# Windowed attention and a gated product: scores issued with values two groups back, weight sums on GpSimd, outputs through other buffers

## The chip, the cores and the metric

The kernel runs on one core of a Trainium2 chip. The metric is the device time of one execution in microseconds (us). Before the change the median of three runs is 662.41 us (660.27 to 663.85). Engines are named as in the profile: PE is TensorE (PEld its weight loads), DVE VectorE, ACT ScalarE, POOL GpSimd, SP SyncE, which issues nearly all DMAs.

## The reference

Attention for 4 batches, 8 heads, 768 positions of 64, with a local window and 24 block summaries, then a gated product of three weights over all 3072 tokens, in float32:

```python
k_sum = k.reshape(B, H, 24, 32, D).max(axis=3)
v_sum = v.reshape(B, H, 24, 32, D).mean(axis=3)
scores_l = where(abs(i - j) < 16, q @ k.T / 8, -1e9)
scores_s = q @ k_sum.T / 8 + log(32)
a = softmax(concatenate([scores_l, scores_s], axis=-1))
attn = a @ concatenate([v, v_sum], axis=2)
x = attn.transpose(0, 2, 1, 3).reshape(3072, 512)
out = ((x @ w_a) * (x @ w_b)) @ w_out        # 512 -> 1536 -> 512
```

## The kernel before

**Numbers in two parts.** TensorE multiplies rounded float32 (`F32R`). Each weight and each activation is kept as a rounded part (hi) and a rest (lo), and a product is three matmuls: hi x hi, lo x hi, hi x lo.

**Chunks.** The tokens form nine chunks u = 0 to 8 of 128-position groups: three of two groups for batch 0, two of three groups for each of batches 1 to 3. For u = 0 to 6 `item(n, u, f)` does one twelfth f of the hidden width: 24 up-products (L1178, 12 for `h0` = x w_a, 12 for `h1` = x w_b, each of 128x384 for a chunk of three groups), then a *gate*: ScalarE copies `h0` to `g` (L1275), VectorE multiplies `h1` by it (L1278), ScalarE rounds that to `gh` (L1280), VectorE forms the rest `gl` (L1283). Nine output products (L1292) follow, six with `gh` and three with `gl`. TensorE does the 24 up-products of the next item before the nine output products of this one.

**Attention of later chunks** (`attention`, `scores`, `transposes`, `products`) runs between items, one group of 128 queries at a time. SyncE loads queries in 16 pieces (`blocks`) into one half of `qin`; VectorE turns them into `qT` (L1122). TensorE forms the scores in banks `c0`, `c1` (L740). VectorE adds the mask (L765) and takes the maximum (L773) into `sbuf`, ScalarE exponentiates (L787), VectorE inverts the sums (L807), GpSimd multiplies by them (L822). VectorE turns the weights into `pbuf` by blocks of 32 (L868). TensorE multiplies by the value window `vbuf` (L890), whose result is split into hi and lo (L934, L938). `lead` joins the value products of a group to the scores of the next one: TensorE does both in one *burst*.

**The last stage** (`whole`) does chunks 7 and 8 together, with seven products of half-size blocks instead of eight. For it `mixtures(f)` forms four sums of weight blocks (T1 to T4) for each of the twelve f: GpSimd adds hi and lo (L1352) and forms sums (L1392), ScalarE rounds them (L1374), GpSimd forms the rest (L1377), and SyncE stores them and three unmixed blocks to `comb` in DRAM (L1336). Two slots, in `S1` and in `late`, are used in turn. Values of chunks 6 to 8 go unrounded to `rawd` or to buffers; `bring_back` loads chunk 6 again and splits it.

**What sets the order.** `Work.emit` plays the operations on a clock of its own with the costs given to `act`, `dve`, `pool`, `pe` and `load`, and issues on each engine the ready operation of the lowest rank. For the first part the order is written out by hand in `ORDER`; an engine's list is followed until it is used up, and operations marked `aside` come only after it. `PLACES` and `MIXED` say at which item a group of attention or a mixture becomes known. On the chip every engine takes its queue strictly in that order.

Of the kernel before, what the change touches and what calls it, by code (L numbers as in the profile page):

```python
# [9 lines left out]
F32 = mybir.dt.float32  # L10
# [59 lines left out]
        434 654-657 660-665 1199 612 638 625 1200 1201 651 669-671 1203 672 1204-1206 717 710  # L70
        675-678 1208 679 680 1209-1211 1213-1216 773 766 1220-1222 1217 1224-1227 827 820
        1229-1232 1234-1237 963 970 1238 1043 1050
# [27 lines left out]
class Work:  # L100
# [10 lines left out]
    def add(self, engine, rank, takes, then, reads, writes, fn, rate=0):  # L111
# [3 lines left out]
            engine=engine, rank=rank, takes=takes, then=then, rate=rate, fn=fn, left=0,  # L115
# [20 lines left out]
    def emit(self):  # L136
# [5 lines left out]
        while any(ready.values()):  # L142
# [34 lines left out]
def attention_moe(  # L177
# [10 lines left out]
    nc = tc.nc  # L188
# [16 lines left out]
    WHOLE, RAW, SPLIT = NU - 2, NU - 3, 5  # L205
# [86 lines left out]
    rawd = dram.tile([3 * WIDE, P, 512], F32, tag="raw", name="rawd")  # L292
# [423 lines left out]
    def scores(u, t, qT, qk, s, sk, banks, diag=None, lead=None):  # L716
# [42 lines left out]
        for h in range(2):  # L759
            if u > FILL:  # L760
                rank = rank_of(u, t) - 0.1 + 0.02 * h
# [15 lines left out]
        for h in range(2):  # L777
            if u > FILL:
                rank = rank_of(u, t) - 0.1 + 0.02 * h
# [3 lines left out]
            for c in range(NP):  # L783
                act(
                    rank, 0.385, [f"{mk}m{h}", xk[h]],
# [42 lines left out]
    def transposes(u, t, s, sk, banks, diag=None):  # L828
# [24 lines left out]
        sv = sbuf.rearrange("p h c x -> p (h c) x")  # L853
# [5 lines left out]
        halves = [slice(0, 4), slice(4, 8)] if u >= SPLIT else [slice(0, 8)]  # L859
# [13 lines left out]
    def products(u, t, vw, vk, bk, pt=None, other=None):  # L873
# [5 lines left out]
        if u >= RAW:  # L879
            other = None  # L880
# [15 lines left out]
        def kept():  # L896
            if u > WHOLE:
                halved(t - chunks[u][1], ps)
                return
            raw, key = slot("S1", 3)  # L900
            act(
                CHAIN, 0.6, [bk], [key],
                lambda: nc.scalar.copy(
                    out=raw.rearrange("p (c a b) -> p c a b", c=NP, a=2),
                    in_=ps.rearrange("p c (b a) -> p c a b", a=2),
                ),
            )
            i = 3 * (u - RAW) + t - chunks[u][1]
            load(80, 262.0, 200, [key], [f"raw.{i}"], rawd[i], raw)
# [42 lines left out]
    SK = ["s0", "s1"]  # L952
    PT = [f"pt{i}{j}" for i in range(4) for j in range(4)]
# [131 lines left out]
    def attention(u):  # L1085
# [4 lines left out]
        if t0 == 0:  # L1090
            prep_keys(b)
            if b < B - 1:
                prep_values(b)
            if b == B - 2:
                work.aside = True
                prep_values(b + 1)
                work.aside = False
# [64 lines left out]

    def later():
        for u in range(FILL + 2, NU):
            yield from attention(u)
        yield
# [32 lines left out]
    def item(n, u, f):  # L1199
# [64 lines left out]
        else:  # L1264
# [5 lines left out]
            for nm, ps, hk in (("a", pa, ak), ("b", pb, bk)):  # L1270
# [6 lines left out]
                CHAIN, 0.08 + W / 1000, [*gk, bk], [bk],  # L1277
# [4 lines left out]
                CHAIN, 0.08 + W / 1000, [bk, ghk], [glk],  # L1282
# [22 lines left out]
        if f == NF - 1:  # L1305
            for j in range(m):
                ob, key = slot("S0" if u < FILL else "S1", j)
                after = CHAIN if u < FILL else 0.5
                if j % 2 == 0:
                    act(after, 0.6, [ok[j]], [key], lambda ob=ob, j=j: nc.scalar.copy(  # L1310
                        out=straight(ob), in_=woven(bank[ok[j]])
                    ))
                else:
                    dve(
                        after, 0.6, [ok[j]], [key],
                        lambda ob=ob: nc.vector.tensor_copy(
                            out=straight(ob), in_=woven(bank[ok[1]])
                        ),
                    )
                row = row0 + j * P  # L1320
                load(90, 262.0, 200, [key], (), out[row : row + P, :], ob)
# [8 lines left out]
    MIXED = [(3, 1), (3, 4), (4, 0), (4, 2), (4, 4), (4, 6), (5, 0), (5, 2), (5, 4), (6, 0), (6, 2), (6, 4)]  # L1330
# [12 lines left out]
    def mixtures(f):  # L1343
        r = [
            spaces["S1"][:, i * 512 : (i + 1) * 512].rearrange("p (h c x) -> p h c x", h=2, c=2)
            for i in range(2)
        ]
        RK = ["S1.0", "S1.1"]
        for i, nm in enumerate("ab"):
            pool(  # L1350
                60, 1.3, weight_key(f, nm), [RK[i], f"go{f}"],
                lambda i=i, nm=nm: nc.gpsimd.tensor_tensor(  # L1352
                    out=r[i].rearrange("p h c x -> p (h c) x"), in0=weight(f, nm)[:, :, 0].bitcast(F32),
                    in1=weight(f, nm)[:, :, 1].bitcast(F32), op=ALU.add,
                ),
            )

        for op, nm in ((B11, "a"), (B21, "a"), (B22, "b")):
            half = op in (B21, B22)
            move(  # L1360
                100, 262.0, 400, weight_key(f, nm) + [f"go{f}"], [f"comb{f}.{op}"], lambda op=op: comb[f][op],
                lambda nm=nm, half=half: flat(f, nm)[:, half * 512 : half * 512 + 512].bitcast(F32),
            )
        def out_part(j, i, h, op):
            def own():
                if j:
                    return late[0][:, 3].rearrange("p c x -> p (c x)")
                return spaces["S1"][:, 1024:1536].bitcast(F32R)

            def w(part):  # L1370
                return own().rearrange("p (c t x) -> p c t x", c=2, t=2)[:, :, part]

            x, key = lambda: r[i][:, h], ["S0.3" if j else "S1.2"]
            act(59, 0.36, [RK[i]], key, lambda: nc.scalar.copy(out=w(0), in_=x()))  # L1374
            pool(
                59, 0.72, [RK[i]], key,
                lambda: nc.gpsimd.tensor_tensor(  # L1377
                    out=w(1), in0=x(), in1=w(0).bitcast(F32), op=ALU.subtract
                ),
            )  # L1380
            move(
                99.5, 262.0, 400, key, [f"comb{f}.{op}"], lambda: comb[f][op],
                lambda: own().bitcast(F32),
            )

        for n, (x, y, z, op, dst) in enumerate((
            ((1, 1), (1, 1), (1, 0), ALU.subtract, T3), ((1, 0), (1, 0), (0, 0), ALU.subtract, T1),
            ((0, 0), (1, 1), (0, 0), ALU.add, T2), ((0, 1), (0, 1), (0, 0), ALU.subtract, T4),
        )):
            pool(  # L1390
                60, 0.72, RK, [RK[x[0]]],
                lambda x=x, y=y, z=z, op=op: nc.gpsimd.tensor_tensor(  # L1392
                    out=r[x[0]][:, x[1]], in0=r[y[0]][:, y[1]], in1=r[z[0]][:, z[1]], op=op
                ),
# [372 lines left out]
```

## Time and profile before

| | |
|---|---|
| median of three runs | 662.41 us |
| profiled execution, its span | 661.2 us, 659.5 us |
| TensorE busy, weight loads busy | 641.8 us (97%), 591.3 us (90%) |
| VectorE, ScalarE, GpSimd busy | 467.0, 275.5, 235.9 us |
| TensorE waiting for `gh` (L1280) | 7.6 us |
| TensorE waiting for transposes (L868) | 2.4 us |

Items of three groups run from about 200 us, the bursts spoken of below from 269 to 513 us, and the last stage from 529 us. A row of a timeline gives start, duration, engine, line and operation, out<-in, the number merged into it, and in brackets the idle time before with what ended it.

### The profile page before, as it was taken

Reading aid. Unit: us, or ns where it says so; the run is one execution under the profiler, and the core shown is the slowest. Engines: PE = TensorE matmul, PEld = TensorE weight load, DVE = VectorE, ACT = ScalarE, POOL = GpSimd, SP = SyncE. Lnnn points to the kernel's source line nnn. Section 1 sums busy time; section 2 is a strip of 40 time slices with the busy share of each in tenths; the row PEclk is TensorE's granted clock in tenths of the full one; section 3 lists DMA queues with packets and bytes.
Section 4 is the critical chain, followed back from the end, with each engine's and each line's share of the span. In section 5 each row is a group of like instructions: output and inputs, shape, how many; then the busy total and the mean of one; then the engine's idle time right before and its main releaser. Section 6 shows DMA issues by size and latency. Waiting matters only on the chain.

```text
span 659.5 us, 13990 instructions
## 1 busy us (share of the span) xinstructions
PE 641.8 (97%) x5064; PEld 591.3 (90%) x5064; DVE 467.0 (71%) x1050; ACT 275.5 (42%) x812; POOL 235.9 (36%) x346
## 2 busy tenths in 40 slices
PE   8999999999999999999999999799999999999997
PEld 6898888899989999998999998699989999999997
DVE  3789988987776694677688865669888645455550
ACT  3996865523533441443345424234454422221120
POOL 6320030246431685357543445214553021212110
PEclk9999999999999999999999999899999999999999
DMA  9999954554433457545345654525546076666620
GB/s 213 266 231 297 335 121 115 125 121 112 117 77 91 115 137 200 128 132 154 125 137 153 175 125 127 149 56 161 176 127 224 11 250 199 197 194 196 198 84 33
DMA packets 184126, 101.98 MB, mean 155 GB/s; under 512 B 138616, under 2 KB 154232, under 8 KB 184056
## 3 DMA queue, kind: packets, MB, share of 16 engines
q1 hardware_dynamic: 183912, 100.95, 56.4%
q8 instruction: 40, 0.66, 0.4%
q14 instruction: 30, 0.25, 0.1%
q10 hardware_dynamic: 144, 0.13, 0.1%
HBM read 71.00 MB, written 30.03 MB: 153 GB/s over the span
## 4 chain that ended last, share of the span: by engine, by line
PE 71%; DVE 15%; SPq 5%; ACT 4%; issue 2%; DMA 2%; POOL 1%; ACTq 0%; DVEq 0%
PE h L1178 29%; PE o L1292 15%; DVE pt L868 10%; PE c L1527 6%; PE h L1527 6%; PE o L1639 5%; SPq L359 4%; PE o L890 3%; PE c L740 2%; PE h L1639 2%; DVE h L1278 2%; ACT s L787 1%; DVE gl L1283 1%; DMA comb<-S 1%; DMA space<-in_q_dram 1%
## 5 line engine op out<-in xcount | busy, mean ns | idle before, releaser
L1178 PE MATMUL h<-x,w 128*128 128x384 f32 (+2 forms) x1608 | 295.7, 320 | 0.1
L1178 PEld LDWEIGHTS h<-x,w 128*128 128x128 f32 x1608 | 253.8, 190 | 9.8 <-issue 1.0
L868 DVE STREAM_TRANSPOSE pt<-s 32x128 f32<-32x128 f32 (+1 forms) x372 | 123.8, 333 | 15.9 <-POOL s L822 9.0
L1292 PE MATMUL o<-w,gh 128*128 128x512 f32 x396 | 100.1, 389 | 7.7 <-ACT gh L1280 7.6
L822 POOL TENSOR_TENSOR s<-s,nml 128x480 f32<-128x480 f32 x40 | 43.8, 1096 | 149.6 <-DVE nml L807 148.3
L1292 PEld LDWEIGHTS o<-w,gh 128*128 128x128 f32 x396 | 72.8, 191 | 19.7 <-ACT gh L1280 10.5
L787 ACT ACTIVATE s<-s,nml 128x120 f32<-128x120 f32 x160 | 61.4, 386 | 21.4 <-DVE nml L773 21.3
L1178 PE MATMUL h<-late,w 128*128 128x384 f32 x192 | 62.8, 327 | 0.0
L1280 ACT CAST gh<-h 128x384 fp32r<-128x384 f32 x48 | 22.9, 476 | 90.9 <-DVE h L1278 90.9
L671 POOL TENSOR_TENSOR S<-S 96x256 f32<-96x256 f32 (+3 forms) x58 | 33.1, 572 | 34.7 <-DMA S<-in_v_dram 26.6
L1292 PE MATMUL o<-w,gl 128*128 128x512 f32 x162 | 45.5, 387 | 0.0
L1278 DVE TENSOR_TENSOR h<-h,g 128x384 f32<-128x384 f32 x48 | 27.0, 563 | 21.4 <-PE h L1178 19.5
L1178 PEld LDWEIGHTS h<-late,w 128*128 128x128 f32 x192 | 36.4, 190 | 0.7
L1392 POOL TENSOR_TENSOR S<-S 128x256 f32<-128x256 f32 x48 | 35.6, 741 | 1.9
L1283 DVE TENSOR_TENSOR gl<-h,gh 128x384 fp32r<-128x384 f32 x48 | 26.4, 550 | 13.7 <-ACT gh L1280 13.0
L1292 PEld LDWEIGHTS o<-w,gl 128*128 128x128 f32 x162 | 30.7, 192 | 5.1 <-issue 0.8
L1592 POOL TENSOR_TENSOR g<-pt,s 128x384 f32<-128x384 f32 x12 | 12.0, 1004 | 63.0 <-ACT s L1579 26.3
L1527 PE MATMUL c<-w,w 128*128 128x384 f32 x180 | 33.8, 326 | 0.0
L1527 PE MATMUL h<-w,w 128*128 128x384 f32 x180 | 33.7, 326 | 0.0
L1352 POOL TENSOR_TENSOR S<-w 128x512 f32<-128x512 f32 x24 | 30.3, 1276 | 7.4 <-DMA out_dram<-S 6.9
L1275 ACT COPY g<-h 128x384 f32<-128x384 f32 x48 | 22.9, 478 | 19.7 <-PE h L1178 19.2
L1527 PEld LDWEIGHTS c<-w,w 128*128 128x128 f32 x180 | 30.3, 189 | 0.7
(213 smaller groups left out, 1031.3 us busy)
## 6 DMA issues: line engine op xcount, KB each, us to landing
w<-comb SPq DMA_DIRECT2D x84, 256.0 KB, 3.0
comb<-w SPq DMA_DIRECT2D x36, 256.0 KB, 2.8
raw<-in_moe_w_a_dram SPq DMA_DIRECT2D x12, 512.0 KB, 6.6
raw<-in_moe_w_out_dram SPq DMA_DIRECT2D x12, 512.0 KB, 6.6
raw<-in_moe_w_b_dram SPq DMA_DIRECT2D x12, 512.0 KB, 7.5
comb<-S SPq DMA_DIRECT2D x24, 256.0 KB, 2.6
comb<-late SPq DMA_DIRECT2D x24, 256.0 KB, 2.4
out_dram<-S SPq DMA_DIRECT2D x22, 256.0 KB, 2.4
```

Of the source, the lines that this page charges most:

```text
L671: lambda: nc.gpsimd.tensor_tensor(out=out, in0=i0, in1=i1, op=ALU.add),
L787: lambda h=h, c=c, sums=sums: nc.scalar.activation(s[h][:, c, :], x[h][:, c, :], AF.Exp, bias=m[:, 0, h, c : c + 1], scale=1.0, accum_out= ...
L822: lambda h=h, r=r: nc.gpsimd.tensor_tensor(out=s[h], in0=s[h], in1=r[:, :, None].broadcast_to([P, NP, KN]), op=ALU.mult,),
L868: lambda js=js, qs=qs, rs=rs: nc.vector.transpose(out=pv[js, rs, qs], in_=sv[qs, rs, js]),
L1178: nc.tensor.matmul(ps, w[:, c, part, :], (xt[:, 4 * xpart : 4 * xpart + 4] if both else inputs_of(u, xpart))[:, :, c].rearrange("p g (a b) ...
L1278: lambda: nc.vector.tensor_tensor(out=pb, in0=pb, in1=g, op=ALU.mult),
L1283: lambda: nc.vector.tensor_tensor(out=gl, in0=pb, in1=gh.bitcast(F32), op=ALU.subtract),
L1292: nc.tensor.matmul(bank[ok[j]], (gh if first else gl)[:, j * P : (j + 1) * P], w[:, :, part, :].rearrange("p (z a) n -> p z n a", a=2), st ...
L1352: lambda i=i, nm=nm: nc.gpsimd.tensor_tensor(out=r[i].rearrange("p h c x -> p (h c) x"), in0=weight(f, nm)[:, :, 0].bitcast(F32), in1=weig ...
L1392: lambda x=x, y=y, z=z, op=op: nc.gpsimd.tensor_tensor(out=r[x[0]][:, x[1]], in0=r[y[0]][:, y[1]], in1=r[z[0]][:, z[1]], op=op),
L1527: nc.tensor.matmul(bank[bk][:, :HT], w[:, c, part, :], x[xpart][:, :, c0 + c].rearrange("p g (a b) -> p g b a", a=2), start=(c, part, xpar ...
L1639: nc.tensor.matmul(bank[bk][:, : nz * CV // 2], gated(x, h)[0][gpart]()[:, js], m, start=(x == 0 and (gpart, part) == (0, 0)), stop=(x == ...
```

## The change

- **Bursts.** For chunks 5 to 8 `groups` takes the place of `attention`. A burst holds the scores of group k and the values of group k-2; the transposes of group k-1 follow it. Softmax has two buffers in turn, `sbuf` and a half of `S1`. In each batch the first scores of the batch have the last values of chunk 4 beside them or none, the second scores have none, and the last two values stand alone. Between bursts inside a batch stand two items; before, two and a half or three. Queries use the first half of `qin` alone. `softmax` and `chunks_of` are small helpers.
- **Transposes** are done in whole rows of 8 blocks, no longer in two halves. Values of chunk 5 are no longer split by key rows.
- **Mixtures.** GpSimd alone forms each sum from the differences of the parts and rounds it; the two slots are used in turn from f = 2 on, one before.
- **Outputs** of chunks 3 to 5 leave through `kin` (first and third group) and the second half of `qin` (second group), which raw values of chunk 7 use as well. Chunk 6's values are split at once; `bring_back` is gone.
- **Planner.** Gates, exponentials and the stores of mixtures get other costs (`slack` delays what another engine does after them), and places and ranks differ. `ORDER` loses the entries of operations that come later.

```diff
@@ Work.emit
+                late = end + (op.slack if o.engine != op.engine else 0.0)
-                o.est = max(o.est, start + op.takes + same if o.engine == op.engine else end)
+                o.est = max(o.est, start + op.takes + same if o.engine == op.engine else late)
@@ attention_moe
-    WHOLE, RAW, SPLIT = NU - 2, NU - 3, 5
+    WHOLE, RAW = NU - 2, NU - 2
@@ scores
-                    rank, 0.385, [f"{mk}m{h}", xk[h]],
+                    rank, 0.575 if u > FILL + 1 else 0.385, [f"{mk}m{h}", xk[h]],
@@ transposes
-        sv = sbuf.rearrange("p h c x -> p (h c) x")
+        sv = (sbuf if sk is SK else sbuf1).rearrange("p h c x -> p (h c) x")
-        halves = [slice(0, 4), slice(4, 8)] if u >= SPLIT else [slice(0, 8)]
+        halves = [slice(0, 4), slice(4, 8)] if False else [slice(0, 8)]
@@ products
-        if u >= RAW:
+        if u > FILL + 2:
             other = None
-            raw, key = slot("S1", 3)
+            raw, key = qin[:, :, P:], "q1.0"
...
+    def softmax(t):
+        if t % 2 == 0:
+            return [sbuf1[:, h] for h in range(2)], ["S1.0", "S1.1"]
+        return s0, SK
...
+    def groups():
+        seq = [(u, i) for u in range(FILL + 3, NU) for i in range(WIDE)]
+        waiting, banks = [], ["c0", "c1"]
...
+        def turned(u, t):
+            b = chunks[u][0]
+            bring(b, t)
+            transposes(u, t, *softmax(t), banks)
+            waiting.append(products(u, t, vbuf, VK, "o3"))
+
+        def direct():
+            reads, bk, fn, split = waiting.pop(0)
+            pe(-1, 1.1, reads, bk, fn)
+            split()
+
+        for k, (u, i) in enumerate(seq):
...
+            for c in range(NP):
+                blocks(98, f"q0.{c}", qin[:, c, :P], q, b, c, t * P)
+            dve(
+                rank_of(u, t) - 0.5, 0.62, [f"q0.{c}.{r}" for c in range(NP) for r in range(0, P, 32)], ["qT"],
+                lambda: nc.vector.transpose(out=qTs, in_=qin[:, :, :P]),
+            )
+            joined = lead.pop() if k == 0 else waiting.pop(0) if t > 1 else None
+            scores(u, t, qTs, "qT", *softmax(t), banks, lead=joined)
+            if t:
+                turned(*(chunks_of(u, t - 1), t - 1))
+            yield
+            if t == S // P - 1:
+                direct()
+                turned(u, t)
+                direct()
...
@@ item
-                CHAIN, 0.08 + W / 1000, [*gk, bk], [bk],
+                CHAIN, 0.56, [*gk, bk], [bk],
...
+                if FILL < u < WHOLE - 1:
+                    ob, key = kin[:, :CV], "kin0.0"
+                if j == 1 and FILL < u < WHOLE - 1:
+                    ob, key = qin[:, :, P:], "q1.0"
...
@@ mixtures
+        def mix(out, x, y, op, reads=()):
             pool(
-                60, 1.3, weight_key(f, nm), [RK[i], f"go{f}"],
+                60, 0.75, reads, [tk],
+                lambda: nc.gpsimd.tensor_tensor(out=out, in0=x(), in1=y(), op=op),
+            )
+        for n, op in enumerate((T1, T3, T2, T4)):
+            if op in (T1, T3):
+                x, y = (("b", 0), ("a", 0)) if op == T1 else (("b", 1), ("b", 0))
+                mix(t, part(*x, 0), part(*y, 0), ALU.subtract, keys)
+                mix(u, part(*x, 1), part(*y, 1), ALU.subtract, keys)
+                mix(t, lambda: t, lambda: u, ALU.add)
+            elif op == T2:
+                mix(u, part("a", 0, 0), part("a", 0, 1), ALU.add, keys)
+                mix(t, lambda: t, lambda: u, ALU.add)
+            else:
+                mix(u, part("a", 1, 0), part("a", 1, 1), ALU.add, keys)
+                mix(t, lambda: u, lambda: t, ALU.subtract)
...
-            act(59, 0.36, [RK[i]], key, lambda: nc.scalar.copy(out=w(0), in_=x()))
+            pool(59, 0.5, [tk], [key], lambda half=half: nc.gpsimd.tensor_copy(out=half(0), in_=t))
...
+            work.ops[-1].slack = 2.0
```

ScalarE around 413 to 426 us of the trace before: L1374 rounds a weight sum into one of the two slots, L1280 is the cast `gh`, L1275 the copy `g`, L903 keeps the values of a group.

```order
L1374 CAST S_191<-S_191 128x2x128
L1280 CAST gh<-h_78 128x384
L1275 COPY g<-h_77 128x384
L1374 CAST late<-S_191 128x2x128
L1280 CAST gh<-h_78 128x384
L903 COPY S_191<-o_76 128x512
L787 ACTIVATE s,nml_172<-s,nml_172 128x120 x4
```

After, at the end of chunk 4 (lines have other numbers there: L1335 is `gh`, L1330 the copy `g`, L934 a rounded value, L1374 the copy of an output into `kin`).

```order
L1335 CAST gh<-h_78 128x384
L1330 COPY g<-h_77 128x384
L934 CAST x<-o_76 128x512
L1335 CAST gh<-h_78 128x384
L1330 COPY g<-h_77 128x384
L934 CAST x<-o_76 128x512
L1374 COPY kin<-o_73 128x512
L1335 CAST gh<-h_78 128x384
L1330 COPY g<-h_77 128x384
L1374 COPY kin<-o_75 128x512
```

No rounding of weight sums stands between the gates; the second copy into `kin` follows the first by three entries.

GpSimd, most of one mixture (f = 5) before: L1352 adds the parts, L1392 forms sums, L1377 the rests, L822 normalises a softmax.

```order
L1352 TENSOR_TENSOR S_191<-w_940 128x512
L1352 TENSOR_TENSOR S_191<-w_995 128x512
L1392 TENSOR_TENSOR S_191<-S_191 128x256
L822 TENSOR_TENSOR s<-s,nml_172 128x4x120 x2
L1377 TENSOR_TENSOR S_191<-S_191 128x2x128
L1392 TENSOR_TENSOR S_191<-S_191 128x256 x2
L1377 TENSOR_TENSOR late<-S_191,late 128x2x128
L1377 TENSOR_TENSOR S_191<-S_191 128x2x128
L1392 TENSOR_TENSOR S_191<-S_191 128x256
```

After, the first half of a mixture (f = 3): L1415 are sums and differences, L1443 the cast into a slot, L1446 the rest, L820 the normalisation.

```order
L1415 TENSOR_TENSOR S_191<-w_899,w_762 128x256 x2
L1415 TENSOR_TENSOR S_191<-S_191 128x256
L1443 CAST late<-S_191 128x2x128
L1446 TENSOR_TENSOR late<-S_191,late 128x2x128
L820 TENSOR_TENSOR s<-s,nml_172 128x4x120
L1415 TENSOR_TENSOR S_191<-w_899 128x256 x2
L1415 TENSOR_TENSOR S_191<-S_191 128x256
L820 TENSOR_TENSOR s<-s,nml_172 128x4x120
L1443 CAST S_191<-S_191 128x2x128
L1446 TENSOR_TENSOR S_191<-S_191 128x2x128
```

The cast into a slot now stands in the same queue as the normalisation, and ahead of it.

VectorE, a group in the middle before: L773 the maximum, L807 the inverse, L868 the transposes, L1278 and L1283 the gate.

```order
L773 TENSOR_REDUCE nml_171<-s 128x4
L1122 STREAM_TRANSPOSE qT<-qin 128x512
L1283 TENSOR_TENSOR gl<-h_78,gh 128x384
L807 RECIPROCAL nml_171<-nml_171 128x4
L868 STREAM_TRANSPOSE pt<-s 32x4x32 x3
L807 RECIPROCAL nml_171<-nml_171 128x4
L868 STREAM_TRANSPOSE pt<-s 32x4x32 x5
L1278 TENSOR_TENSOR h_78<-h_78,g 128x384
L868 STREAM_TRANSPOSE pt<-s 32x4x32 x3
L1283 TENSOR_TENSOR gl<-h_78,gh 128x384
L868 STREAM_TRANSPOSE pt<-s 32x4x32 x13
```

After, a group of batch 3 (L763 mask, L771 maximum, L805 inverse, L866 transposes, L1204 the queries, L1333 and L1338 the gate).

```order
L763 SCALAR_TENSOR_TENSOR S_191<-c_79,mask 128x4x120
L771 TENSOR_REDUCE nml_171<-S_191 128x4
L763 SCALAR_TENSOR_TENSOR S_191<-c_80,mask 128x4x120
L771 TENSOR_REDUCE nml_171<-S_191 128x4
L866 STREAM_TRANSPOSE pt<-s 32x8x32 x3
L1333 TENSOR_TENSOR h_78<-h_78,g 128x384
L805 RECIPROCAL nml_171<-nml_171 128x4
L1204 STREAM_TRANSPOSE qT<-qin 128x512
L1338 TENSOR_TENSOR gl<-h_78,gh 128x384
L866 STREAM_TRANSPOSE pt<-s 32x8x32 x4
```

The transposes between the gates read the other buffer (`s`) than the scores just masked (`S`).

## Rows read from the trace of the kernel before

**Rows 1.** Windows, 275 to 526 us: busy us by engine, clock, DMA share, GB/s.

```profile
275.00:526.00 251.00, 240.74 (x2010) 222.61 (x2010) 191.68 (x511) 107.25 (x365) 107.97 (x128) 0.99 0.47 137
```

**Rows 2.** Waits of PE: us in total, times, longest us.

```profile
PE o L1292 <- ACT gh L1280: 7.6, 8, 4.4
PE o L890 <- DVE pt L868: 2.4, 5, 0.6
```

**Rows 3.** Timeline, 413 to 426 us, SP and ACT.

```profile
413.29 9.65 SPq L359 DMA_DIRECT2D qin<-in_q_dram  x16
...
423.04 0.38 SPq L1336 DMA_DIRECT2D comb<-late  x1
...
425.30 0.40 ACT L1374 CAST late<-S 128x256 fp32r<-128x256 f32 x1 [9.90 <-DMA comb<-late]
```

**Rows 4.** Chain that ended last: start us, us, what.

```profile
402.88 1.08 PE o L890 x32
403.96 0.98 PE c L740 x32
...
426.14 4.21 PE o L1292 x9
430.34 4.21 PE h L1178 x24
...
445.13 2.14 PE o L1292 x9
447.27 3.90 PE h L1178 x24
451.17 1.94 PE o L1292 x9
```

**Rows 5.** Timeline, PE, a split burst's first product and the next work.

```profile
307.62 0.27 PE L890 MATMUL o<-pt,vw 64*64 64x64 f32 x1
...
309.53 0.48 PE L1292 MATMUL o<-w,gl 128*128 128x512 f32 x1
```

**Rows 6.** Windows, the eight long bursts: their sum.

```profile
sum 20.33, PE 17.75 PEld 15.12 DVE 12.48 ACT 7.85 POOL 5.85; mean PE 2.22 PEld 1.89 DVE 1.56 ACT 0.98 POOL 0.73
```

**Rows 7.** Groups by line and shape, POOL: busy us, mean ns, idle before.

```profile
L1392 POOL TENSOR_TENSOR S<-S 128x256 f32<-128x256 f32 x48 | 35.6, 741 | 1.9
L1352 POOL TENSOR_TENSOR S<-w 128x512 f32<-128x512 f32 x24 | 30.3, 1276 | 7.4 <-DMA out_dram<-S 6.9
...
L1377 POOL TENSOR_TENSOR S<-S 128x256 fp32r<-128x256 f32 x24 | 17.5, 729 | 36.4 <-ACT S L1374 36.4
...
L962 POOL CAST space<-mask 128x256 fp32r<-128x256 f32 x1 | 0.4, 397 | 0.0
```

**Rows 8.** Groups by line and shape, DVE, transposes.

```profile
L868 DVE STREAM_TRANSPOSE pt<-s 32x128 f32<-32x128 f32 x288 | 87.2, 303 | 13.5 <-POOL s L822 8.6
L868 DVE STREAM_TRANSPOSE pt<-s 32x256 f32<-32x256 f32 x84 | 36.6, 436 | 2.4 <-PE o L890 0.6 <-POOL s L822 0.4
```

**Rows 9.** Timeline, DVE, a run of transposes.

```profile
299.85 5.12 DVE L868 STREAM_TRANSPOSE pt<-s 32x128 f32<-32x128 f32 x16
```

**Rows 10.** Timeline, SP, the shortest run of 16 query loads seen.

```profile
314.26 7.45 SPq L359 DMA_DIRECT2D qin<-in_q_dram  x16
```

**Rows 11.** Groups by line and shape, DVE, the gate.

```profile
L1278 DVE TENSOR_TENSOR h<-h,g 128x384 f32<-128x384 f32 x48 | 27.0, 563 | 21.4 <-PE h L1178 19.5 <-ACT nml L803 1.2
L1283 DVE TENSOR_TENSOR gl<-h,gh 128x384 fp32r<-128x384 f32 x48 | 26.4, 550 | 13.7 <-ACT gh L1280 13.0
```

**Rows 12.** Timeline, DVE and POOL, differences of two SBUF inputs.

```profile
493.73 2.05 POOL L1392 TENSOR_TENSOR S<-S 128x256 f32<-128x256 f32 x2
...
495.11 2.83 DVE L1414 TENSOR_TENSOR w<-inW,w 128x256 fp32r<-128x256 f32 x5
...
515.28 1.76 DVE L1414 TENSOR_TENSOR w<-inW,w 128x256 fp32r<-128x256 f32 x5
```

**Rows 13.** Timeline, POOL, second normalisation after the burst at 402.88.

```profile
411.78 0.99 POOL L822 TENSOR_TENSOR s<-s,nml 128x480 f32<-128x480 f32 x1 [1.26 <-DVE nml L807]
```

More of the change, by code (lines that the diff above doesn't have):

```diff
@@ L114, in add @@
         op = SimpleNamespace(
-            engine=engine, rank=rank, takes=takes, then=then, rate=rate, fn=fn, left=0,
+            engine=engine, rank=rank, takes=takes, then=then, rate=rate, fn=fn, left=0, slack=0.0,
             est=0.0, next=[], index=self.extra if self.aside else self.count,
@@ L1091, in attention @@
             prep_keys(b)
[L1092 to L1097, printed above, removed]
+            prep_values(b)
         if u == FILL:
@@ L1343, in mixtures @@
     def mixtures(f):
[L1344 to L1349, printed above, removed]
-            pool(
-                60, 1.3, weight_key(f, nm), [RK[i], f"go{f}"],
-                lambda i=i, nm=nm: nc.gpsimd.tensor_tensor(
-                    out=r[i].rearrange("p h c x -> p (h c) x"), in0=weight(f, nm)[:, :, 0].bitcast(F32),
-                    in1=weight(f, nm)[:, :, 1].bitcast(F32), op=ALU.add,
-                ),
-            )
+        t, u = (spaces["S1"][:, i : i + 256].rearrange("p (c x) -> p c x", c=2) for i in (1024, 1280))
@@ new lines, in mixtures, with part, own, half @@
+        tk = "S1.2"
+        def part(nm, h, x):
+            return lambda: weight(f, nm)[:, 2 * h : 2 * h + 2, x].bitcast(F32)
+        def mix(out, x, y, op, reads=()):
+            pool(
+                60, 0.75, reads, [tk],
+                lambda: nc.gpsimd.tensor_tensor(out=out, in0=x(), in1=y(), op=op),
+            )
+        keys = weight_key(f, "a") + weight_key(f, "b")
+        for n, op in enumerate((T1, T3, T2, T4)):
[10 more added lines that the diff above has]
+                mix(t, lambda: u, lambda: t, ALU.subtract)
+            j = n % 2 if f > 1 else 0
+            def own(j=j):
+                if j:
+                    return spaces["S1"][:, 1536:].bitcast(F32R)
+                return late[0][:, 3].rearrange("p c x -> p (c x)")
+            def half(x, own=own):
+                return own().rearrange("p (c t x) -> p c t x", c=2, t=2)[:, :, x]
+            key = ("S0.3", "S1.3")[j]
+            pool(59, 0.5, [tk], [key], lambda half=half: nc.gpsimd.tensor_copy(out=half(0), in_=t))
+            pool(
+                59, 0.75, [tk], [key],
+                lambda half=half: nc.gpsimd.tensor_tensor(
+                    out=half(1), in0=t, in1=half(0).bitcast(F32), op=ALU.subtract
+                ),
+            )
+            work.ops[-1].slack = 1.0
+            move(
+                99.5, 262.0, 400, [key], [f"comb{f}.{op}"], lambda op=op: comb[f][op],
+                lambda own=own: own().bitcast(F32),
+            )
+            work.ops[-1].slack = 2.0
@@ L1358, in mixtures @@
+        work.add("-", 0, 0, 0, [tk], [f"go{f}"], lambda: None)
         for op, nm in ((B11, "a"), (B21, "a"), (B22, "b")):
-            half = op in (B21, B22)
+            h = op in (B21, B22)
             move(
                 100, 262.0, 400, weight_key(f, nm) + [f"go{f}"], [f"comb{f}.{op}"], lambda op=op: comb[f][op],
[L1362 to L1373, printed above, removed]
-            act(59, 0.36, [RK[i]], key, lambda: nc.scalar.copy(out=w(0), in_=x()))
[L1375 to L1394, printed above, removed]
-            )
-            out_part(n % 2, *x, dst)
```

81 lines of the change are left out of this document (46 added, 35 removed), and 12 rows, old and new, of the table ORDER.

## The prediction

> **What bounds the kernel now.** I read the busy time of the stretch in question first, then TensorE's own waits, then the places where it stood longest, and last the prices on the engines that feed it. TensorE is the bound: from 275 to 526 us it works 240.74 of 251.00 us [rows 1]. So only two things can move the time: TensorE's own work, and the 10.3 us of idle time in this stretch, with what the clock loses there. The waits say who causes it: 7.6 us of the output products (L1292) waiting for ScalarE's cast `gh`, once for 4.4 us, and 2.4 us of the value products (L890) waiting for VectorE's transposes [rows 2].
>
> The 4.4 us have a clear history [rows 3]. SyncE issues 16 query loads in a row for 9.65 us; the store of a weight sum (`comb<-late`) stands behind them and goes out at 423.04. ScalarE takes its queue in order and waits 9.90 us for that landing before it may round the next weight sum; the cast `gh` that TensorE needs is the next entry. After the idle time the clock is at its lower level (1.2 GHz instead of 2.4): nine output products and the 24 up-products behind them take 4.21 and 4.21 us, where 2.14 and 3.90 are normal behind a burst [rows 4]. That is 2.07 + 0.31 = 2.4 us more.
>
> The bursts (values of a group and scores of the next) hold a third loss. An undisturbed one lasts 1.08 + 0.98 = 2.06 us [rows 4], or 1.91 us (307.62 to 309.53) where the values are split by key rows [rows 5]. Eight bursts, one of them split and the last with values alone, last 20.33 us together [rows 6]; undisturbed they would take 1.91 + 6 x 2.06 + 1.08 = 15.35. The excess is 5.0 us, of which the list of waits names 2.4; the rest are pauses inside a burst while transposes trickle in.
>
> **The change part by part.**
>
> *Weight sums off ScalarE.* The 48 rounding casts leave ScalarE, and with them its waits for these stores. One mixture on GpSimd is now 2 x 1.276 + 4 x 0.741 + 4 x 0.729 = 8.4 us. After, it is 10 sums of 256 columns, 4 casts and 4 differences: 10 x 0.741 + 4 x 0.397 + 4 x 0.729 = 11.9 us [rows 7] (0.397 is another 128x256 cast on GpSimd). Twelve mixtures cost GpSimd 42 us more. It worked 107.97 of 251.00 us [rows 1], so it has room, and none of this is on TensorE's path as long as the softmax normalisation, which shares its queue, is in time.
>
> *Two softmax buffers, values two groups late.* Today a group's transposes follow its own softmax and precede the next burst: one long chain. After, the transposes behind burst k belong to group k-1, whose softmax has had a whole interval. So VectorE no longer stands waiting for GpSimd, and the excess of the bursts goes. The transposes go back from 24 halves of 303 ns to 12 wholes of 436 ns [rows 8], 7.27 to 5.23 us a group, and the longest run without a gate between them falls from 16 halves, 5.12 us [rows 9], to some six wholes, 2.6 us. Such runs make `gh` late and explain most of the smaller entries among the 7.6 us.
>
> *TensorE's own work.* The matmuls are the same but for the values: three groups lose the split by rows (3 x 0.15 = 0.45 us), and there are three bursts more, because in each batch the second scores and the last values stand alone. Leaving a burst costs up to 2.14 - 1.94 = 0.2 us [rows 4]; I take the middle, 0.1 each. In all +0.75 us.
>
> *SyncE.* Between bursts stand two items instead of two and a half or three: 2 x 3.90 + 2.14 + 1.94 + 2.06 = 13.9 us. In this time SyncE issues 16 query loads (7.45 to 9.65 us [rows 3, 10]), three value loads at the same 0.47 to 0.60 each, and about seven stores at 0.38 [rows 3]: 11.5 to 14.1 us. The low end fits, the high end doesn't quite. Queries have one buffer half instead of two; it is free as soon as VectorE has turned it, a whole interval ahead of its next use. Bounds: 0, and 0.2 us for each of eight such bursts; I take 1.0, nearer the dear end, because that row stood ahead of the worst stall.
>
> *Outputs through `kin` and `qin`.* The third copy of a chunk's output writes the buffer of the first, so ScalarE waits for a store again, at three chunk ends. If the store goes at once, 3.90 us of up-products cover it; behind 16 query loads ScalarE would be up to 9.65 us late and TensorE some 5.7, each time. I take 1.0 us in all, near the low end: in SyncE's order a store has at most eight query loads directly ahead.
>
> *Chunk 6's store and return* (three stores, loads, casts, differences) go: they lie beside TensorE's work, 0.
>
> *GpSimd beside VectorE.* GpSimd's longer mixtures now reach into the time when VectorE forms the sums for the last stage. A gate is 0.563 + 0.550 us of VectorE's [rows 11]. Five differences of two SBUF inputs take 1.76 us while GpSimd is idle, 0.35 each, and 2.83 us at 495.11 beside two GpSimd operations, whose two sums before take 2.05 instead of 1.48 [rows 12]: 1.07 us more, 0.53 for each meeting. After, 12 such operations stand in a row between two gates: 4.2 us alone, 10.6 if each meets one. An item leaves VectorE 5.84 - 1.11 = 4.7 us, and the up-products ahead of the output products give some 2.3 more, 7.0 in all. So the price is 0 to 3.6 us; I take 2.0, since GpSimd is busy but not without gaps. The Trainium skill's page "SBUF — State Buffer", section "Who interferes with whom", has the rule: a VectorE instruction with two SBUF inputs and a GpSimd instruction that reads SBUF exclude each other, and the second waits in full. The trace agrees (0.35 against 0.88). By the rule, with each of the 12 waiting out one whole sum of 0.741, the row takes 13.1 us and the price is 6.1; and GpSimd's other 42 us are free, because transposes, reductions and gates have at most one SBUF input.
>
> **Sum.** It is made against the profiled execution, 661.2 us (span 659.5 and 1.7 around it); the median of the runs, 662.41, is 1.2 above. -7.6 (output products) - 2.4 (clock) - 5.0 (bursts) + 0.75 (TensorE's work) + 1.0 (SyncE) + 1.0 (outputs) + 2.0 (contention) = -10.25, or 650.95. With the 1.2 for the median: **652.2 us**. This case alone runs from 648 to 657.
>
> **Rivals.**
>
> *Slower: SyncE sets the pace.* The place are the eight bursts at a distance of two items. Value loads wait until TensorE has read the value windows, and queries stand behind them in SyncE's queue. With the dear loads, 14.1 us, and such a wait of 1.6 us a group, SyncE needs 15.7 of 13.9 us: 1.8 us late at each of eight bursts, 14.4 us, and once an idle time that lowers the clock, 2.4 us: 652.2 + 16.8 = 669 us. It tips the verdict from 1.7 us a burst. For it: the 9.65 us ahead of the worst stall. Against it: the cheap row of 16, and six items without a burst after a batch, in which SyncE can catch up.
>
> *No change: the wait moves to GpSimd.* GpSimd's cast needs the slot of the store before last. If that store stands behind 16 query loads, up to 9.65 us, the normalisation behind it in GpSimd's queue is late, then the transposes, then the burst. Today a softmax is through 412.77 - 404.94 = 7.8 us after its burst [rows 4, 13]; the slack is 13.9 - 2.06 - 7.8 = 4.0 us, the stall 5.6, and the clock takes 2.4: 660 us with one such place. For it: the same stores in the same queue. Against it: two slots used in turn, and VectorE comes to these transposes only after the next burst.
>
> *Little gained: contention.* Each of the 12 meets GpSimd, 1.6 us more than taken, and 2 us in the smaller groups of sums around: 656 us. For it: the lengthened rows at 495. Against it: only a few mixtures are left by then.
>
> **How the numbers follow.** Forecast 0.62, SyncE's pace 0.13, the wait on GpSimd 0.13, contention 0.12. About 0.5%, 3.3 us, is what a measurement of this kernel can tell from no change. Faster takes the forecast and most of contention, 0.72; same the GpSimd case and the rest, 0.15; slower SyncE's pace, 0.13. The range begins where nothing new is paid (661.2 - 15.0 + 0.75 = 647) and ends just above the GpSimd case, 662; SyncE's pace and small tails stay outside.
>
> **What would show it.** Right: TensorE's idle time between 275 and 526 falls from 10 us to under 5, with no granted clock below full there; `gh` all but leaves TensorE's waits; whole bursts last 2.06 us; ScalarE waits for no `comb` store. Wrong: TensorE waiting for `qT` with `qin` loads behind it (SyncE); transposes waiting for a normalisation while GpSimd waits for `comb` (the moved wait); differences of 0.9 us ahead of a late gate in the last chunk (contention); ScalarE standing on `out_dram<-kin`.

## The result: slower, where the forecast was faster

The changed kernel takes 664.19 us (median of 20 runs), the kernel before 660.66 us (20 runs): ratio 1.0059, 95% interval 1.004 to 1.0078. The forecast was some 10 us less (652.2), with a range of 647 to 662. The time lies outside it, on the other side. All times given here are of fast runs: one run of e8 (2338 us) and one of e10 (1339 us) were slow and are left out.

### The profile page after: what moved, and what is told of

It is laid out like the page before. It is cut to its first block, busy times and chain, and to the rows that moved or that the text cites. A ratio compares the mean times of both kernels' runs of the same rounds, so it can differ in the third digit from the quotient of the medians.

```text
span 662.9 us, 13673 instructions
## 1 busy us (share of the span) xinstructions
PE 641.4 (97%) x4968; PEld 591.7 (89%) x4968; DVE 450.3 (68%) x903; ACT 255.4 (39%) x758; POOL 277.6 (42%) x442
## 4 chain that ended last, share of the span: by engine, by line
PE 75%; DVE 8%; SPq 8%; DMA 4%; issue 2%; POOL 1%; ACT 1%; DVEq 0%; POOLq 0%; ACTq 0%
PE h L1233 32%; PE o L1347 17%; SPq L357 7%; PE h L1581 6%; PE c L1581 6%; PE o L1693 5%; DVE pt L866 3%; PE o L888 2%; PE c L738 2%; PE h L1693 2%; DMA space<-in_v_dram 1%; DMA qin<-in_q_dram 1%; DVE w L1468 1%; DMA space<-in_q_dram 1%; DVE inW L1546 1%
## 5 line engine op out<-in xcount | busy, mean ns | idle before, releaser
L1233 PE MATMUL h<-x,w 128*128 128x384 f32 (+2 forms) x1608 | 297.5, 321 | 1.4 <-DVE gl L1338 1.2
L1233 PEld LDWEIGHTS h<-x,w 128*128 128x128 f32 x1608 | 254.6, 191 | 11.8 <-DVE gl L1338 1.8
L1347 PE MATMUL o<-w,gh 128*128 128x512 f32 x396 | 100.5, 390 | 11.9 <-ACT gh L1335 11.9
L1347 PEld LDWEIGHTS o<-w,gh 128*128 128x128 f32 x396 | 72.9, 191 | 23.0 <-ACT gh L1335 13.2
L820 POOL TENSOR_TENSOR s<-s,nml 128x480 f32<-128x480 f32 x28 | 31.8, 1137 | 137.9 <-DVE nml L805 105.8
L866 DVE STREAM_TRANSPOSE pt<-s 32x256 f32<-32x256 f32 x156 | 68.0, 436 | 9.5 <-PE o L888 2.8
L1335 ACT CAST gh<-h 128x384 fp32r<-128x384 f32 x48 | 22.9, 478 | 129.2 <-DVE h L1333 123.4
L1233 PE MATMUL h<-late,w 128*128 128x384 f32 x192 | 62.7, 326 | 0.0
L1333 DVE TENSOR_TENSOR h<-h,g 128x384 f32<-128x384 f32 x48 | 27.1, 565 | 52.2 <-PE h L1233 50.3
L785 ACT ACTIVATE s<-s,nml 128x120 f32<-128x120 f32 x112 | 43.0, 387 | 18.7 <-DVE nml L771 18.7
L1347 PE MATMUL o<-w,gl 128*128 128x512 f32 x162 | 45.8, 389 | 0.3 <-DVE gl L1338 0.3
L1415 POOL TENSOR_TENSOR S<-w 128x256 f32<-128x256 f32 x58 | 43.1, 755 | 1.1
L1233 PEld LDWEIGHTS h<-late,w 128*128 128x128 f32 x192 | 36.3, 189 | 0.6
L1415 POOL TENSOR_TENSOR S<-S 128x256 f32<-128x256 f32 x48 | 35.3, 736 | 3.3
L1347 PEld LDWEIGHTS o<-w,gl 128*128 128x128 f32 x162 | 31.2, 195 | 5.8 <-DVE gl L1338 1.1
L866 DVE STREAM_TRANSPOSE pt<-S 32x256 f32<-32x256 f32 x72 | 31.4, 436 | 6.9 <-POOL S L820 2.6
L1330 ACT COPY g<-h 128x384 f32<-128x384 f32 x48 | 22.9, 478 | 29.9 <-PE h L1233 29.9
L1338 DVE TENSOR_TENSOR gl<-h,gh 128x384 fp32r<-128x384 f32 x48 | 26.4, 551 | 10.0 <-ACT gh L1335 8.1
```

The source lines that it names most:

```text
L785: lambda h=h, c=c, sums=sums: nc.scalar.activation(s[h][:, c, :], x[h][:, c, :], AF.Exp, bias=m[:, 0, h, c : c + 1], scale=1.0, accum_out= ...
L820: lambda h=h, r=r: nc.gpsimd.tensor_tensor(out=s[h], in0=s[h], in1=r[:, :, None].broadcast_to([P, NP, KN]), op=ALU.mult,),
L866: lambda js=js, qs=qs, rs=rs: nc.vector.transpose(out=pv[js, rs, qs], in_=sv[qs, rs, js]),
L1233: nc.tensor.matmul(ps, w[:, c, part, :], (xt[:, 4 * xpart : 4 * xpart + 4] if both else inputs_of(u, xpart))[:, :, c].rearrange("p g (a b) ...
L1333: lambda: nc.vector.tensor_tensor(out=pb, in0=pb, in1=g, op=ALU.mult),
L1338: lambda: nc.vector.tensor_tensor(out=gl, in0=pb, in1=gh.bitcast(F32), op=ALU.subtract),
```

## The profile after

First the answers to [rows 1] and [rows 2], for the changed kernel: TensorE is L1233 (up-products), L1347 (output products), L888 (values), L738 (scores); `gh` is L1335, transposes L866, the gate's halves L1333 and L1338, the queries' transposition L1204.

```profile
275.00:526.00 251.00, 238.43 (x1910) 221.03 (x1903) 178.05 (x368) 91.22 (x322) 154.54 (x234) 0.98 0.49 137
```

```profile
PE o L1347 <- ACT gh L1335: 11.9, 4, 7.0
...
PE h L1233 <- DVE gl L1338: 1.2, 2, 1.0
...
PE o L888 <- DVE pt L866: 0.4, 1, 0.4
```

The first row is the stretch from 275 to 526 us, the waits are those of the whole run. The waits for transposes are all but gone as forecast (0.4 us for 2.4), and of eight waits for `gh` four are left. But three of these are long: 7.0, 3.4 and 1.2 us. In the stretch TensorE stands 12.6 of 251 us, for 10.3 before.

The bursts are whole. A part of the chain that ended last (start us, us, what):

```profile
308.92 1.08 PE o L888 x32
310.00 0.98 PE c L738 x32
310.98 2.14 PE o L1347 x9
```

That is 2.06 us. Of nine bursts of both parts, eight last 2.06 and one 2.65; the eight long ones of before had 2.5 on average [rows 6]. Counted back from the last up-product, the 24 that start at 468.94 before start at 462.00 after: the change is 6.9 us ahead. The next 24 start at 474.79 before and 481.01 after: 6.2 behind. Of the 13.2 us between, 4.2 are a burst and nine output products that stand there after and elsewhere before; the other 9.0 are one idle time and the slow products behind it. The timeline there (start us, us, engine, line, operation; idle time before in brackets):

```profile
454.07 0.91 SPq L357 DMA_DIRECT2D rawd<-qin  x1
...
458.29 0.33 SPq L1398 DMA_DIRECT2D inW<-rawd  x1
...
458.71 8.16 SPq L357 DMA_DIRECT2D qin<-in_q_dram  x16
...
466.98 0.38 SPq L357 DMA_DIRECT2D vw<-in_v_dram  x1
...
468.35 0.71 DVE L1204 STREAM_TRANSPOSE qT<-qin 128x512 f32<-128x512 f32 x1 [7.09 <-DMA qin<-in_q_dram]
469.07 0.89 DVE L866 STREAM_TRANSPOSE pt<-s 32x256 f32<-32x256 f32 x2
...
469.99 0.57 DVE L1333 TENSOR_TENSOR h<-h,g 128x384 f32<-128x384 f32 x1
...
470.59 0.48 ACT L1335 CAST gh<-h 128x384 fp32r<-128x384 f32 x1 [5.90 <-DVE h L1333]
...
471.12 2.93 PE L1347 MATMUL o<-w,gh 128*128 128x512 f32 x6 [7.00 <-ACT gh L1335]
```

Read it from the bottom. TensorE waits for `gh`, that for the gate, and the gate stands in VectorE's queue behind the queries' transposition, whose loads land at 468. These loads went out late, because SyncE stood from 454.98 to 458.29: it had stored raw values to `rawd` and had to read the same values back (`inW<-rawd`) next, so it waited for the store to land. It had done the same at 445.2. Its list of waits between 425 and 470 us (us in total, times, longest):

```profile
SPq L1398 <- DMA rawd<-qin: 6.3, 2, 3.2
```

The second place is in the last chunk, where VectorE forms sums (L1546) and differences (L1468) for the last stage:

```profile
503.98 4.11 DVE L1468 TENSOR_TENSOR w<-inW,w 128x256 fp32r<-128x256 f32 x5
504.73 1.67 POOL L1415 TENSOR_TENSOR S<-w 128x256 f32<-128x256 f32 x2
...
509.74 0.55 DVE L1333 TENSOR_TENSOR h<-h,g 128x384 f32<-128x384 f32 x1
...
510.99 1.86 PE L1347 MATMUL o<-w,gh 128*128 128x512 f32 x6 [3.36 <-ACT gh L1335]
```

Five differences take 4.11 us beside GpSimd's mixture, 0.82 each; in [rows 12] they took 0.35 alone. The chain that ended last shows what the clock adds behind both places:

```profile
471.12 3.90 PE o L1347 x9
...
510.99 3.14 PE o L1347 x9
514.13 4.65 PE h L1233 x24
```

Normal are 2.14 us for the nine behind a gap or a burst, 1.94 without, and 3.90 for the 24 [rows 4]. The granted clock is 0.54 from 470 to 475 us, near the lower of its two levels (1.2 and 2.4 GHz), and 0.71 from 510 to 515. So the first place costs 7.00 + 1.76 = 8.8 us and the second 3.36 + 1.00 + 0.75 = 5.1 us. Two smaller ones are new: 1.24 us at 270, where the burst that had covered the first gate of chunk 4 now comes behind it, and 1.00 us at 441, which began with another qT that waited ahead of `gl`.

## The experiments

All but one start from the changed kernel (664.19; ratio to before 1.0059). Ratios are to the kernel before, with their intervals. My theory: SyncE's queue makes the queries late at 464, VectorE's order turns that into a late gate, and GpSimd's company makes the gate at 508 late. Rivals: the wait has moved to GpSimd, which stands up to 9.60 us for `comb` stores and has the softmax behind it; or the loss is one that returns elsewhere when it is mended. In e5, e11 and e2, which leave work out, every other queue keeps the order of the changed kernel.

**e1, the gate first.** The planner is told that the last group's queries land 6 us later:

```diff
+                blocks(98, f"q0.{c}", qin[:, c, :P], q, b, c, t * P); work.ops[-1].slack = 6.0 * ((u, i) == (NU - 1, 2))
```

> The changed kernel, but the transposition of the last group's queries (qT, L1204) stands behind one gate on VectorE instead of ahead of it; nothing else moves on TensorE, GpSimd or SyncE. My theory: TensorE's stall of 7.00 us at 464 comes from this one place, where VectorE waits 7.09 us for query loads and the gate stands behind. Then the stall goes below 1 us and with it the 1.8 us of lower clock behind it: about 8.8 us less than the changed kernel, near 655.4 us against 660.7 before (ratio near 0.992). Rival 1, GpSimd's wait of 9.60 us for a comb store makes the softmax and so the whole row late: the stall stays above 4 us and the time above 661. Rival 2, given back: the stall goes at 464 but the burst behind it now waits for qT and transposes: 659 to 662.

660.33 us, ratio 0.9997 (0.9977 to 1.0016): 3.9 us less than the changed kernel, not 8.8. The stall is gone, and more than half comes back at the next burst:

```profile
457.33 8.58 SPq L357 DMA_DIRECT2D qin<-in_q_dram  x16
466.01 0.38 SPq L357 DMA_DIRECT2D vw<-in_v_dram  x1
...
468.74 0.34 PE L888 MATMUL o<-pt,vw 120*64 120x64 f32 x4 [1.11 <-DMA vw<-in_v_dram]
470.98 1.03 PE L888 MATMUL o<-pt,vw 120*64 120x64 f32 x28 [1.90 <-DMA vw<-in_v_dram]
```

What the burst waits for are its value loads, which stand behind the 16 query loads. Rival 2 was right on the time, but the burst waits for value loads, not for `qT` and transposes: the cause of the return is SyncE again.

**e4, the round trip planned.** A load that reads back a store counts as ready when the store has landed, no longer 0.6 us after its issue:

```diff
-                o.est = max(o.est, start + op.takes + same if o.engine == op.engine else late)
+                o.est = max(o.est, start + op.takes + same if o.engine == op.engine and not op.trip else late)
@@ kept
+            ); work.ops[-1].trip = True
```

> The changed kernel with one rule of the planner changed: a load that reads back what a store of raw values (rawd) has just written is no longer planned 0.6 us after it, but after its landing. SyncE then stands 2 x 3.2 us less on inW<-rawd, and comb stores, value loads and 13 of 16 query loads go ahead of it. My theory: SyncE's round trip makes the queries late; they land some 4 to 6 us earlier, and the stall of 7.00 us goes below 2: 6 to 8.8 us less, 655.5 to 658. Rival: the loads themselves are too many for the time between two bursts (SyncE sets the pace); then the stall stays above 4 us and the time above 660.

658.92 us, ratio 0.9970 (0.9954 to 0.9987), 5.3 us less, short of the 6 to 8.8 expected. The stall falls from 7.00 to 2.24 us, not below 2, and what is left has another cause:

```profile
462.83 0.62 ACT L1465 CAST x<-inW 128x512 fp32r<-128x512 f32 x1 [5.46 <-DMA inW<-rawd]
...
466.00 1.22 PE L1347 MATMUL o<-w,gh 128*128 128x512 f32 x2 [2.24 <-ACT gh L1335]
```

Now ScalarE waits 5.46 us for the raw values, which are read back behind 13 query loads, and `gh` stands behind that cast and the exponentials that follow it. The run is no clean test of the round trip: with the new landing time the planner also put the gate ahead of the queries' transposition on VectorE (461.92 and 466.84 us), as in e1.

**e5, no query loads for the last group.**

```diff
+                lambda: rank == 98.5 or nc.sync.dma_start(out=out, in_=in_), rate=rate,
@@ groups (rank 98.5 for the last group's queries)
```

> The changed kernel without the 16 query loads of the last group of batch 3 (left out: its scores are made with older queries). Nothing else moves in any queue. Theory: SyncE is the pace at 464 us; without 8.2 us of its issuing neither qT nor the value loads behind the queries are late, so the whole stall of 7.00 us and the 1.8 us of lower clock go and, other than with the gate put first, nothing is given back at the next burst: 8.8 us less than the changed kernel, near 655.4. Rival (the softmax is late by GpSimd's wait of 9.6 us for a comb store, and the next burst waits for it): about 4 us less, near 660, as with the gate first.

656.45 us, ratio 0.9934 (0.9912 to 0.9955), 7.7 us less. The 7.00 us are 0.69, the next burst doesn't wait, and nothing is given back:

```profile
465.28 1.56 PE L1347 MATMUL o<-w,gh 128*128 128x512 f32 x6 [0.69 <-ACT gh L1335]
...
469.37 1.15 PE L888 MATMUL o<-pt,vw 120*64 120x64 f32 x32
470.45 1.05 PE L738 MATMUL c<-kT,qT 64*64 64x120 f32 x32
```

**e11, GpSimd without mixtures** (`f in (0, 2) and` ahead of each of its three operations).

> The changed kernel with GpSimd's part of all mixtures but f = 0 and f = 2 left out; the stores stay. It takes away GpSimd's waits for comb stores (9.6 us ahead of the softmax at 453) and all its company of VectorE. Theory: GpSimd matters only beside the differences at 504 to 515, and SyncE's queue makes the 7.00 us; so the stall at 464 stays above 5 us and the time is that without the last two mixtures, 660 to 661. Rival (the wait moved to GpSimd): the stall at 464 falls below 3 us and the time to 653 to 657.

660.00 us, ratio 0.9992 (0.9975 to 1.0009). GpSimd works 49 us between 275 and 526, for 155, and waits for no `comb` store; the wait at 464 is still 6.8 us:

```profile
PE o L1347 <- ACT gh L1335: 8.0, 2, 6.8
```

So GpSimd's waits for `comb` don't make this stall: that rival falls. The time is within 1 us of that of e2, which leaves out the last two mixtures alone.

**e2, no late mixtures** (`f < 10 and` ahead of the same operations).

> The changed kernel without GpSimd's sums, casts and rests of the last two mixtures (f = 10, 11), which are left out; their stores stay and carry old contents. My theory: the gate at 508 is late because GpSimd lengthens VectorE's differences. Without GpSimd's work five of them in a row take about 2.1 us instead of 4.1, the wait of 3.36 us goes below 0.5 and the 1.75 us of lower clock behind it go: about 5 us less, near 659 us. Rival: the row of 12 sums between two gates is too long by itself; then the differences are shorter but over 1.5 us of the wait stay, near 662.

660.93 us, ratio 0.9999 (0.9985 to 1.0014), 3.3 us less for 5 expected. The row of differences is shorter, and the wait falls to 0.73 us with the granted clock at 1.00 behind it, the higher level; the 24 up-products take their normal 3.9 us again. The first stall, at 464, is 7.4 us in this execution. GpSimd still does a cast and a rest of an earlier mixture beside the first row of differences; the next row has no company and takes the 1.76 us of [rows 12]:

```profile
504.41 2.49 DVE L1468 TENSOR_TENSOR w<-inW,w 128x256 fp32r<-128x256 f32 x5
...
508.87 1.56 PE L1347 MATMUL o<-w,gh 128*128 128x512 f32 x6 [0.73 <-ACT gh L1335]
...
509.34 1.76 DVE L1468 TENSOR_TENSOR w<-inW,w 128x256 fp32r<-128x256 f32 x5
```

**e6, the same by order alone.** The planner is told 0.9 us for each sum and difference, so that at most six stand between two gates:

```diff
-            rank, 0.1 + n / 1000, [xk, hk], [lk],
+            rank, 0.1 + n / 1000 + 0.5 * (n == 2 * P), [xk, hk], [lk],
@@ inputs_
-                        rank + 0.01 * j, 0.36, ks_, [ko],
+                        rank + 0.01 * j, 0.9, ks_, [ko],
```

> The changed kernel with one pair of planner costs changed: the sums and differences for the last stage (L1546, L1468 of 256 columns) cost 0.9 us instead of 0.36, which is what they take beside GpSimd. At most 5 to 6 of them then stand between two gates instead of 12. Theory: the gate at 508 is on time, wait 3.36 and clock 1.75 go, 3.5 to 5 us less than the changed kernel: 659 to 660.7. Rival: the sums now end later and the last stage's first products wait for them, by 2 us or more: 662 to 664.

659.95 us, ratio 0.9993 (0.9977 to 1.0010), 4.2 us less. The differences still take 0.8 us each, but the gate now waits for TensorE and not TensorE for it:

```profile
506.38 0.57 DVE L1333 TENSOR_TENSOR h<-h,g 128x384 f32<-128x384 f32 x1 [2.60 <-PE h L1233]
...
507.96 2.38 DVE L1468 TENSOR_TENSOR w<-inW,w 128x256 fp32r<-128x256 f32 x3
```

**e3 and e9, both places at once.**

> Both edits above at once (the last two mixtures on GpSimd left out as there). If the two are the places where my forecast failed, and they are independent, the two gains add up: 8.8 + 5.1 = 13.9 us less than the changed kernel, near 650.3 us, ratio to before near 0.984, beside the 652.2 of my forecast. Rival: another loss is shared or takes their place; then over 655.

e3 is e1 with e2: 655.97 us, ratio 0.9931 (0.9909 to 0.9953), 8.2 us less, near the sum of e1 and e2 (3.9 + 3.3). The 650.3 of the theory is missed and the time is on the rival's side (over 655), since e1's gain is the half one.

> The changed kernel without the last group's 16 query loads and without GpSimd's work on the last two mixtures (both left out). If the two places are all that parts the changed kernel from my forecast, their gains add: 7.7 + 3.3 = 11.0 us by the medians so far, 653.2 us, and 9.6 + 4.3 = 13.9 at most by the traces, 650.3. That would be 7.5 to 10.4 us under before, where the forecast had 10.25. Rival (a third loss as large as these): 656 or more.

e9 is e5 with e2: 652.73 us, ratio 0.9877 (0.9845 to 0.9910), 0.5 us from the sum of the medians. With the two places taken away the changed kernel is 8.1 us faster than before. A third loss of their size there isn't.

**e7, one part alone, on the kernel before:** GpSimd rounds the weight sums.

```diff
-            act(59, 0.36, [RK[i]], key, lambda: nc.scalar.copy(out=w(0), in_=x()))
+            pool(59, 0.5, [RK[i]], key, lambda: nc.gpsimd.tensor_copy(out=w(0), in_=x()))
```

> The kernel before with one part of the change alone: the 48 casts that round the weight sums are done by GpSimd instead of ScalarE. Theory (terms one and two of my forecast): ScalarE no longer waits for comb stores, the stall of 4.4 us at 421 and its 2.4 us of lower clock go, and some of the smaller gh waits: 6 to 9 us less than before, 652 to 655. Rival (the wait moves to GpSimd): the softmax behind GpSimd's cast is late by the same store, bursts wait for transposes, and at most 3 us are left: 657.5 to 661.

658.01 us, ratio 0.9953 (0.9937 to 0.9969): 2.9 us less than before. That is the time of the rival (at most 3), not the 6 to 9 of the theory. Its waits of TensorE:

```profile
PE o L1292 <- ACT gh L1280: 4.7, 8, 1.0
PE o L890 <- DVE pt L868: 2.6, 5, 0.7
```

The 4.4 us and the lower clock are gone (granted clock 1.00 from 275 to 526), as the theory has it. But TensorE's other waits for `gh` are longer than before (4.7 us in eight, for 7.6 - 4.4 = 3.2 in seven), so taking the casts off ScalarE doesn't shorten them. Bursts wait hardly longer than in [rows 2] (2.6 us for 2.4): the rival's time was right, its mechanism not. The gain is under the 4.4 + 2.4 us that went: the other waits grew by 1.5 us, and in this execution TensorE is 1.6 us behind the trace before already at 65 us, with the same order of work; whether other executions lose that too isn't known.

**e8, e10, e12: mends of the order.** e8 has the edits of e1, e4 and e6. e10 and e12 (one kernel, measured twice) plan the queries of batch 3's other groups 2 us later as well:

```diff
+                blocks(98, f"q0.{c}", qin[:, c, :P], q, b, c, t * P); work.ops[-1].slack = 3.0 * (2 if (u, i) == (NU - 1, 2) else 0.667 * (u >= NU - 2))
```

> The changed kernel with three mends at once: landing of raw stores planned, the last qT behind its gate, and differences costed 0.9 us. If the losses are the places named, the gains add: 5.2 us (landing planned) + 1 to 3 (rest of the stall at 464) + 3.5 to 5 (gate at 508): 651.5 to 654.5, ratio to before 0.987 to 0.991. Rival: they share one cause or the next wait takes their place: 656 or more.

654.66 us, ratio 0.9906 (0.9881 to 0.9931): just above the range that I gave. 2.0 us are left at 465 and 1.4 at the next burst.

> The version with all three mends, and the queries of the other groups of batch 3 planned 2 us later as well, so that no qT of that batch stands ahead of both halves of a gate with its loads out. Theory: the 1.0 us at 441 and part of the 2.0 at 465 go: 1 to 3 us less than with three mends (655.3): 652.5 to 654.5. Rival: bursts move and wait for later queries: 655 or more.

651.47 us (three runs), ratio 0.9855 (0.9813 to 0.9897): 3.2 us under e8, a little more than expected.

> The version of e10 again, with more rounds and for its profile. If the median of its three runs holds, 650 to 653.5 us, ratio 0.984 to 0.990; TensorE's idle time between 275 and 526 us under 3 us, no wait for gh over 1 us but the 1.24 at 270, and the granted clock full throughout. Rival: it was a lucky few runs; then 654 or more and a wait at 465 of 2 us or more, as with the three mends alone.

651.43 us, ratio 0.9864 (0.9838 to 0.9890). It beats both kernels, with the work of the changed one and another order. From 275 to 526 us TensorE stands 2.05 us, with the clock full (first row). The waits for `gh` in the whole run (second row) have the 1.2 us at 270 as their longest:

```profile
275.00:526.00 251.00, 248.95 (x1986) 232.04 (x1986) 182.89 (x380) 94.28 (x328) 161.72 (x243) 1.00 0.52 149
```

```profile
PE o L1347 <- ACT gh L1335: 2.1, 3, 1.2
```

## Why the prediction was wrong, step by step

By spans the change is 662.9 - 659.5 = 3.4 us dearer, where the sum had -10.25. The terms:

| term of the sum | forecast | measured |
|---|---|---|
| waits for `gh` with old causes, clock behind | -10.0 | gone |
| excess of bursts | -5.0 | all but 0.6 gone |
| TensorE's own work | +0.75 | not measured by itself |
| SyncE | +1.0 | +8.8 (7.00 and 1.76 clock, at one burst) |
| contention in the last chunk | +2.0 | +5.1 (3.36 and 1.75 clock) |
| outputs through `kin` and `qin` | +1.0 | 0 (ScalarE waits 2.8 us in all for `kin`, under cover) |
| not foreseen | 0 | +1.24 at 270, +1.00 at 441, +0.75 in three small gaps |

Put in for the forecast terms, these give -10.25 + 0.6 + 7.8 + 3.1 - 1.0 + 3.0 = 3.25, near the 3.4 us.

The trace before already had the kind of wait that the sum leaves out: SyncE stands until a store to `rawd` has landed, three times and 9.6 us in all, the longest shortly ahead of the 16 query loads of [rows 3]:

```profile
SPq L1336 <- DMA rawd<-S: 9.6, 3, 3.9
```

```profile
404.87 0.40 SPq L359 DMA_DIRECT2D rawd<-S  x1
409.22 0.34 SPq L1336 DMA_DIRECT2D x<-rawd  x1
```

- **"In all +1.0" for SyncE is the step that failed.** The count of its issues was near: the time between two bursts was tight, as computed. Two things were missing. SyncE doesn't only issue, it also stands for landings: `inW<-rawd` behind `rawd<-qin` holds its queue 3.2 us, twice in 15 us, and the planner counts such a pair at 0.6 us. One such wait added to my count of 11.5 to 14.1 us makes 14.7 to 17.3, for 13.9 between two bursts. And my upper bound (0.2 us at each of eight bursts) took late queries to delay a burst. They delayed the gate behind them in VectorE's queue, with no cover. I asked what stands behind the new waits for stores, and not what stands behind the queries' transposition. In the kernel before it had parts of a gate behind it as well, but VectorE never waited there for these loads; after, it does so three times, 8.9 us in all.
- **"SyncE sets the pace"**, the slower rival at 0.13, had the right queue, but another cause (value loads that wait for TensorE, where the runs show round trips) and the wrong shape: not 1.8 us at each of eight bursts, but once, where two round trips meet. e5 shows that it is the pace there, e1 that a mend on VectorE alone gives half back to it.
- **"I take 2.0" for contention** was mis-sized. Differences of 0.82 to 0.95 us were near the forecast's 0.88, and the lateness of 3.36 us near its upper end of 3.6; but the clock fell behind that idle time, and the 1.75 us of that weren't in the bound. The rule of the Trainium skill ("SBUF — State Buffer", "Who interferes with whom") would have priced it at 6.1. Its direction holds here: in e2 the five fall from 4.11 to 2.49 us, with two GpSimd operations left beside them, and the next five take 1.76 with none. Its size doesn't: a difference gains 0.5 us beside a sum of 0.74, not the whole of it, so the prediction's "the trace agrees (0.35 against 0.88)" holds for the direction alone.
- **"GpSimd has room" held.** e11 leaves out nearly all its mixtures and gains hardly more than e2 (4.2 us for 3.3). GpSimd waits up to 9.60 us for `comb`, as the second rival had it; VectorE's transposes wait for a normalisation six times, 1.5 us at most, and TensorE's own waits for transposes come to 0.4 us.
- **The first term held in sum, its reason in part.** The 4.4 us and the clock behind them went with the casts, as e7 shows. The smaller `gh` waits didn't; they went only with the rest of the change, whose parts (bursts, transposes) no run separates.
- e12 comes out 9.5 us under before, near the forecast's 10.25 under its own execution. So what the change removes was sized about right, in sum; the order that the planner made of it cost 13 us against that of e12.

## What to carry to other kernels

Where the order of queues is fixed ahead, take each instruction that waits for a DMA and ask what stands behind it on its engine: a late load costs what that is worth, not what its own user is worth. Count a queue's waits for landings (a store that is read back) with its issues, since they block like issues. And price an idle time of TensorE with the clock that may fall behind it; here 7.0 us cost 8.8 and 3.4 us cost 5.1.

## What the runs showed of the hardware

- Reading back what a store to DRAM has just written held SyncE's queue for 3.2 us after the issue of the store, twice; the 16 query loads behind it took another 8.16 us.
- Contention of VectorE and GpSimd is paid by both: differences of 256 columns take 0.35 us alone and 0.82 in the row of five beside GpSimd, GpSimd's sums 0.79 to 0.91 instead of 0.74.
- Behind 3.36 us of idle time TensorE lost 1.75 us to the lower clock, behind 1.24 us at 270 nothing: the nine output products there take their 2.14 us. The loss isn't fixed by the length: at the second place e5 stands 2.94 us and keeps the granted clock at 1.00 (the nine output products take 2.21 us); e1 stands 2.95 us, and the granted clock from 505 to 510 us is 0.66 (they take 3.90). No run shows what decides.
